# Beacon attention and soft-MoE slots on one core: pair 2's scores before the first attends, the tail's PSUM tiles, a weight load and dummy matmuls moved

## The chip, the cores and the metric

One NeuronCore of a Trainium2 chip runs the whole program. The metric is the time of one execution on the device in microseconds. Six executions of the kernel before took 194.52 to 196.42 us, with a median of 196.32. One execution was profiled; its trace gives the start and length of every instruction and every transfer.

## The reference

Causal attention with 16 beacon keys in front, for 8 batches of 8 heads, followed by a soft mixture of experts over all 4608 tokens:

```python
# q, k, v: (8, 8, 576, 64); beacon_k, beacon_v: (8, 8, 16, 64), float32
k_all = np.concatenate([beacon_k, k], axis=2)
v_all = np.concatenate([beacon_v, v], axis=2)
scores = scale * np.matmul(q, k_all.transpose(0, 1, 3, 2))
scores = np.where(causal, -1000000000.0, scores)      # beacons are never masked
a = softmax(scores)                                    # over the keys
x = np.matmul(a, v_all)                                # -> (4608, 512): tokens, heads * 64
logits = x @ phi                                       # phi (512, 32): 8 experts * 4 slots
d = softmax(logits, axis=0)                            # over the tokens (dispatch)
slot_input = (d.T @ x).reshape(8, 4, 512)
for e in range(8):
    h = np.maximum(slot_input[e] @ w1[e], 0.0)         # w1 (8, 512, 1024)
    slot_out[e] = h @ w2[e]                            # w2 (8, 1024, 512)
c = softmax(logits, axis=1)                            # over the slots (combine)
out = c @ slot_out.reshape(32, 512)                    # (4608, 512) float32
```

## The kernel before

The schedule is written by hand: each engine runs its instructions in the order of the program text, and waits are placed where tiles overlap. The unit of work is a pair of heads: 32 pairs, `n` from 0 to 31, four pairs (`g` = 0 to 3) to a batch `b`.

**One pair.** `load_pair` (L90) reads q and k of a pair as float32, 288 KB each, on SP's queue, into one of five slots; pair `m + 5` is issued (`load_more`, L407) as soon as PE has turned pair `m`. `transp(n, i)` (L253) turns q (`i` = 0) or k (`i` = 1) with 18 small PE transposes into a `tr` tile of PSUM, of which there are two, and a copy brings it to `qT` or `kT`: DVE (L271) or, for k of pairs 0, 2, 3, 4 and 7, ACT (L269). The first 16 columns of `kT` are the pair's beacon keys from `bkT` (L256 on ACT, L258 on DVE or POOL); `beacons` (L242) makes `bkT`, for batch 0 ahead of the loop and for the others at n = 3, after POOL has doubled them (L205).

`score(n, st)` (L275) computes the transposed scores of a pair in four steps into the PSUM tiles `scs[0]` and `scs[1]` by turns; ACT takes the exponential into `ex[n]` (L289) and POOL zeroes the causal triangle (L291). `attend_blocks` (L298) multiplies 15 blocks of `ex` for each head with v and a column of ones, which gives the sums of the softmax, into the PSUM tile `av`: head 0 in its first half, head 1 in its second. `normalize` (L310) is a reciprocal (L314) and a multiplication (L315) on DVE, into `xb`. `xt_piece` (L333) turns `xb` back through a `tr` tile into `xT`, copied by DVE (L343). `logit_piece` (L345), `dt_piece` (L359) and `si_products` (L383) are the routing of a finished batch: logits and their exponential, its transposition, and the sums for the slots.

**v and the weights** go through POOL's queue as casting loads to float16: v in pieces of 32 partitions (`load_v` L112, `load_tail` L143), the experts' weights in 32 pieces of 512 KB (`load_w` L176). DVE turns v (`turn_v` L154, `turn_tail` L158, both L151) before it can be used. POOL's DMA semaphores come round every eight loads: a load waits until the one eight before it has landed. POOL runs its loads and its affine selects in one order. Of the weights, one piece follows at the end of each iteration as `want` (L540) says: none at n = 0, then one each at n = 1 to 5, none at n = 6.

**The loop's order.** An iteration is `score(n, 0)`, `score(n, 1)`, the attend of head 0 of an earlier pair, `score(n, 2)`, the turning of k of the next pair, `score(n, 3)`, the attend of head 1 and `normalize`. In the first iterations the attends lag by two pairs; at n = 4 two pairs are attended and the lag becomes one. `transp(m, 0)` of the next q stands after `score(n, 1)` up to n = 4 and after `score(n, 0)` from n = 5 on. At n = 4 and 5 two `xt_piece` follow each other (L463). `warm` (L237) issues dummy matmuls on a tile that nobody reads: six and two ahead of the loop, two at n = 1, four at n = 2.

**The tail** (from L553). The last pair's heads are attended in `scs[0][:, 0]` and `av[:, 1]`, each normalized by itself (`normalize_head`, L320). Then come the last logits (L564) into `scs[1]`, the folding of the slots' sums (`fold_si`, L398) into `scs[0][:, 1]`, `col_sums` (L420), which adds the combine weights of a token into columns of `av[:, 0]`, three dummies (L582), `dt_piece`, and the slots' inputs into `siz`. The experts run in four steps of two experts: `first_layer(p)` (L609) into `scs[0][:, 0]` or `av[:, 1]` by turns and a relu on ACT (L618), `turn_hidden(p)` (L620) with a copy on DVE (L624), `second_layer(p)` (L626) into `sop`, which is `av[:, 0]`. At p = 1 `col_sums(7, NG)` and its factors on DVE (L549, L551) follow. `soh` (L648) scales the result, and 37 matmuls (L660) with copies by ACT and DVE write the output, 9.4 MB on SP's queue.

Of the kernel before, what the change touches and what calls it, by code (L numbers as in the profile page):

```python
# [17 lines left out]
def kernel(  # L18
# [190 lines left out]
        load_v(0, qd)  # L209
    for i in range(3):  # L210
        load_tail(0, i)
    idh = const.tile([P, P], F16, name="idh")
    ones = const.tile([P, 1], F16, name="ones")
    nc.vector.memset(ones[:, :], 1.0)
# [80 lines left out]
    def attend_head(n, a):  # L295
        attend_blocks(n, a, av[:, a, :], [(c, i) for i in range(NCH) for c in range(i + 1)])
# [10 lines left out]
                vchunk(b, 2 * g + a, c, kn),  # L307
                start=(c == 0), stop=(c == i))

    def normalize(n):  # L310
        b, g = divmod(n, H // 2)
        r5 = sml.tile([P, 2, NCH], FP, name="r5", tag="r5")
        avv = av[:, :, 0:NCH * DD].rearrange("p a (i d) -> p a i d", d=DD)
        nc.vector.reciprocal(out=r5[:, :, :], in_=avv[:, :, :, D])  # L314
        nc.vector.tensor_tensor(  # L315
            out=xb[b % 2][:, :, 2 * g:2 * g + 2, :].rearrange("p i a d -> p a i d"),
            in0=avv[:, :, :, 0:D],
            in1=r5[:, :, :].unsqueeze(3).broadcast_to([P, 2, NCH, D]), op=AL.mult)

    def normalize_head(n, a, src):  # L320
        b, g = divmod(n, H // 2)
        r5 = sml.tile([P, NCH], FP, name="r5h", tag="r5h")
        avv = src[:, 0:NCH * DD].rearrange("p (i d) -> p i d", d=DD)
        nc.vector.reciprocal(out=r5[:, :], in_=avv[:, :, D])
        nc.vector.tensor_tensor(
            out=xb[b % 2][:, :, 2 * g + a, :], in0=avv[:, :, 0:D],
            in1=r5[:, :].unsqueeze(2).broadcast_to([P, NCH, D]), op=AL.mult)

    xT = {}
    dT = {}  # L330

    def xt_piece(n):
        b, g = divmod(n, H // 2)  # L333
        if g == 0:
            xT[b] = exq.tile([P, NDC, U], F16, name="xT", tag="xT", bufs=2)
        tp = ps_tr.tile([P, NCH, P], F16, name="tr", tag="tr")
        for i in range(NCH):
            m = P if i < 4 else UL
            nc.tensor.transpose(  # L339
                tp[:, i, 0:m],  # L340
                xb[b % 2][0:m, i, 2 * g:2 * g + 2, :].rearrange("p h d -> p (h d)"),
                idh[0:m, 0:m])
        nc.vector.tensor_copy(out=xT[b][:, g, :],  # L343
                              in_=tp[:, :, :].rearrange("p i u -> p (i u)")[:, 0:U])

    def logit_piece(b, hf):
        lp = ps_tr.tile([P, 512], FP, name="tr", tag="tr")
# [49 lines left out]

    def fold_si(h):  # L398
        if h == 0:
            fsp[0] = scs[0][:, 1, 0:NDC * NSL].rearrange("p (c s) -> p c s", c=NDC)  # L400
        for c in (2 * h, 2 * h + 1):
            x = siacc[:, 256 * h:256 * h + 256].rearrange("p (f r) -> p f r", r=2)
            nc.tensor.matmul(fsp[0][:, c, :], x[:, :, c % 2], fold[:, :], start=True, stop=True)
        if h == 1:
            nc.vector.tensor_copy(out=siT[:, :, :], in_=fsp[0])
# [25 lines left out]
    transp(0, 1)  # L431
    warm(1)
    nc.vector.tensor_copy(out=idh[:, :], in_=idb[:, :])
    wl = 0
    for n in range(NP):
        b, g = divmod(n, H // 2)
        score(n, 0)
        m = n + 1 if n < 6 else n + 2
        if 5 <= n and m < NP:
            transp(m, 0)  # L440
        if n == NP - 1:
            dt_piece(b - 1)
        score(n, 1)
        if n == NP - 1:
            add_si(si_products(b - 1))
        if n < 5:
            transp(m, 0)
        for x, y in {1: ((0, 0), (0, 1)), 3: ((1, 1),), 4: ((1, 0), (1, 2)), 6: ((2, 0), (2, 1)),
                     7: ((2, 2),), 8: ((2, 3),)}.get(n, (divmod(n + 3, 4),) if n > 8 else ()):
            if x < B:  # L450
                turn_v(x, y)
        if 13 <= n < 17:
            turn_tail(1, n - 13)
        if n == 2:
            warm(4)
        if 2 <= n < 5:
            attend_head(n - 2, 0)
        elif n >= 5:
            if n >= 8 and g == 0:
                col_sums(b - 2, b - 1)  # L460
            attend_head(n - 1, 0)
        if n >= 4:
            for x in {4: (0, 1), 5: (2, 3)}.get(n, (n - 2,)):  # L463
                xt_piece(x)
        score(n, 2)
        if n == 3:
            beacons(1, B)
        if m < NP:
            if n == 1:
                warm(2)  # L470
            transp(m, 1)
            if n > 0:
                load_more(m)
        score(n, 3)
        if n == 0:
            hold(3)
            load_pair(3)
            nc.sync.dma_start(out=bkf[:, 1:B, :], in_=bks[:, 1:B, :])
            load_pair(4)
            load_more(0)  # L480
            load_more(1)
            nc.sync.dma_start(out=phif[:, :, :], in_=moe_phi.rearrange("(c p) e -> p c e", p=P))
        if n == 0:
            load_v(1, 0)
        if n == 1:
            for y in range(1, 4):
                load_v(1, y)
            turn_v(0, 2)
            turn_v(0, 3)
            for y in range(4):  # L490
                turn_tail(0, y)
        if n >= 2:
            x = n - 2 if n < 5 else n - 1
            attend_head(x, 1)
            normalize(x)
        if n == 4:
            turn_v(1, 3)
            attend_head(3, 0)
            attend_head(3, 1)
            normalize(3)  # L500
        if n == 5:
            for i in range(2):
                transp(7, i)
            load_more(7)
        if 6 <= n < NP - 1 and g == 3:
            dt_piece(b - 1)
        if n >= 5 and g in (1, 2):
            logit_piece(b - 1, g - 1)
        if n >= 8 and g == 0:
            add_si(si_products(b - 2))  # L510

        if n == 4:
            nc.gpsimd.tensor_copy(out=phih[:, :, :, :],
                                  in_=phif[:, :, :].unsqueeze(2).broadcast_to([P, NDC, 4, NSL]))
        if n == 2:
            for r in range(2):
                double_beacons(nc.gpsimd, r, 1, B)
        if n == 12:
            nc.gpsimd.memset(siz[:, :, :, :], 0.0)
        if n == 16:  # L520
            nc.gpsimd.tensor_copy(out=fold[:, :], in_=idb[:, 0:NSL])
            for z in range(1, 4):
                nc.gpsimd.tensor_tensor(out=fold[:, :], in0=fold[:, :],
                                        in1=idb[:, NSL * z:NSL * z + NSL], op=AL.add)
            nc.gpsimd.tensor_scalar(out=fold[:, :], in0=fold[:, :], scalar1=2.0 ** -8,
                                    scalar2=None, op0=AL.mult)
        if n == 3:
            for qd in range(4):
                load_v(2, qd)
        if n == 4:  # L530
            load_bv(2)
        x, y = divmod(n - 4, 4)
        if n >= 4 and x + 3 < B:
            for qd in ((0,), (1, 2), (3,), ())[y]:
                load_v(x + 3, qd)
            if y == 2:
                load_bv(x + 3)
        if 8 <= n < 11:
            load_tail(1, n - 8)
        want = n if n < 6 else n - (n - 2) // 4 if n < 24 else 18 + 9 * (n - 23) // 5  # L540
        while wl < min(want, NPC):
            load_w(wl)
            wl += 1
# [8 lines left out]

    L = B - 1  # L553

    avl = [scs[0][:, 0, :], av[:, 1, :]]
    for a in range(2):
        attend_blocks(NP - 1, a, avl[a], [(c, 4) for c in range(NCH)])
    xt_piece(NP - 2)
    for a in range(2):
        attend_blocks(NP - 1, a, avl[a], [(c, i) for i in (3, 2, 1, 0) for c in range(i + 1)])  # L560
        normalize_head(NP - 1, a, avl[a])
    lps = [scs[1][:, hf, 0:S // 2] for hf in range(2)]

    def last_logits(ts):  # L564
# [4 lines left out]
                                 xT[L][:, t, o:o + S // 2],  # L569
                                 start=(t == 0), stop=(t == NDC - 1))  # L570

    last_logits(range(NDC - 1))
    fold_si(0)
    xt_piece(NP - 1)
    fold_si(1)
    last_logits([NDC - 1])
    for hf in range(2):
        o = Nb + L * S + hf * (S // 2)
        nc.scalar.activation(eLh[:, o:o + S // 2], lps[hf], AF.Exp)
    col_sums(6, 7)  # L580
    for _ in range(3):
        nc.tensor.matmul(scs[0][:, 1, :], idh[:, :], xT[L][:, 0, 0:512], start=True, stop=True)  # L582
    dt_piece(L)
    ds = siz[:, :, :, :]
    for hf in range(2):
        sp = si_half(L, hf)
# [20 lines left out]
    EP = E // 2  # L607

    def first_layer(p):  # L609
        hp = av[:, 1, :] if p % 2 else scs[0][:, 0, :]  # L610
        for c in range(NDC):
            for z in range(4):
                e = 2 * p + z // 2
# [21 lines left out]
    for p in range(EP + 2):  # L635
        if p < EP:
            first_layer(p)
        if 0 < p <= EP:
            turn_hidden(p - 1)
        if p == 1:  # L640
            col_sums(7, NG)
            col_sum_factors()
        if p > 1:
            second_layer(p - 2)
    soh = const.tile([P, Dm], F16, name="soh")
# [55 lines left out]
```

The softmax here doesn't subtract the row's maximum and nothing guards it: scores larger than these inputs give would overflow.

## Time and profile before

| | us |
|---|---|
| median of 6 runs | 196.32 |
| lowest and highest | 194.52, 196.42 |
| profiled execution | 196.42 |
| its span, first to last instruction | 194.7 |
| PE busy | 157.3 |
| DVE busy | 137.6 |
| ACT busy | 129.0 |
| POOL busy | 111.1 |

Busy times are those of one engine within the span; they overlap, so they don't add up to it. Of PE, matmuls and weight loads are counted apart (weight loads 104.6 us). The granted clock of PE was 0.961 of full speed in the mean. The transfers read 62.65 MB and wrote 9.44 MB. The chain that ended last, by engine:

```profile
PE 62%; DVE 10%; DMA 7%; issue 6%; POOL 3%; ACT 3%; SPq 1%; DVEq 0%
```

"issue" is time in which an engine waited for nothing that the profile shows, and a q after an engine's name is its queue. The loop runs from about 6.5 us to 149 us, the routing and the experts of the tail to 166.7 us, the output to the end. Loads take long to land since many are under way at once, which the page's list of issues shows (size of one, median from issue to landing):

```profile
arena<-in_moe_w_dram POOLq DMA_DIRECT2D x32, 512.0 KB, 9.3
arena<-in_q_dram SPq DMA_DIRECT2D x32, 288.0 KB, 12.8
arena<-in_k_dram SPq DMA_DIRECT2D x31, 288.0 KB, 13.5
```

### The profile page before, as it was taken

The page shows a single profiled execution, that of the slowest core. Times are in us where ns is not written, and L with a number is a line of the kernel's source. Part 1 is how long each engine was busy: PE and PEld are TensorE (multiplying, and loading weights), DVE is VectorE, ACT ScalarE, POOL GpSimd, SP SyncE. Part 2 cuts the span into 40 slices and gives each one's busy share as a digit, 9 for nine tenths or more (in the row PEclk, how much of TensorE's full clock was granted, in tenths as well). Part 3 has the DMA queues.
Part 4 walks back from the last instruction along what each step waited for, and adds up shares of the span by engine and source line. Part 5 has one row for each costly group of instructions (what it writes and reads, how often), then busy time and mean ns, then how long its engine had stood idle before and what let it go on. Part 6 is the DMA issues. An engine that isn't in the chain of part 4 may idle for free.

```text
span 194.7 us, 7200 instructions
## 1 busy us (share of the span) xinstructions
PE 157.3 (81%) x3063; PEld 104.6 (54%) x3065; DVE 137.6 (71%) x286; ACT 129.0 (66%) x189; POOL 111.1 (57%) x285
## 2 busy tenths in 40 slices
PE   6668857899997999999899998988987889787000
PEld 2435645677575766666676775666655654332000
DVE  5573397889986899899788899877755552699000
ACT  2793964698696788878977987887896122499000
POOL 8687675868788598659957876666756200000000
PEclk9996999999999999999999999999999999999755
DMA  5999999999999999999999999999999980199995
GB/s 198 266 265 349 251 296 291 257 263 260 308 267 263 257 287 292 263 282 296 253 271 266 276 260 280 236 220 216 215 216 210 204 163 3 56 403 417 416 426 226
DMA packets 20464, 50.84 MB, mean 261 GB/s; under 512 B 5456, under 2 KB 5456, under 8 KB 19408
## 3 DMA queue, kind: packets, MB, share of 16 engines
q0 software_dynamic: 8048, 21.74, 56.6%
q1 hardware_dynamic: 12240, 28.35, 39.6%
q8 instruction: 24, 0.39, 0.7%
q10 hardware_dynamic: 144, 0.29, 0.5%
q14 instruction: 8, 0.07, 0.1%
HBM read 62.65 MB, written 9.44 MB: 370 GB/s over the span
## 4 chain that ended last, share of the span: by engine, by line
PE 62%; DVE 10%; DMA 7%; issue 6%; POOL 3%; ACT 3%; SPq 1%; DVEq 0%
PE av L304 18%; PE sc L282 15%; PE tr L265 11%; DVE arena L664 4%; PE tr L339 4%; DMA arena<-in_moe_w_dram 4%; DMA arena<-in_k_dram 3%; PE tr L350 3%; DVE xb L315 2%; PE av L629 2%; PE tr L388 2%; ACT ex L289 1%; POOL ex L291 1%; PE av L422 1%; PE sc L615 1%
## 5 line engine op out<-in xcount | busy, mean ns | idle before, releaser
L289 ACT ACTIVATE ex<-sc 128x736 f16<-128x736 f32 (+1 forms) x124 | 101.9, 868 | 24.7 <-PE sc L282 23.1
L291 POOL TENSOR_SCALAR_AFFINE_SELECT ex<-ex 128x256 f16<-128x256 f16 (+1 forms) x155 | 57.6, 401 | 33.8 <-ACT ex L289 33.2
L282 PE MATMUL sc<-qT,kT 64*128 64x336 bf16 (+5 forms) x384 | 45.4, 287 | 5.4 <-POOL kT L258 1.2
L304 PEld LDWEIGHTS <-ex 128*128 128x128 f16 (+1 forms) x930 | 35.8, 106 | 17.6 <-issue 16.8
L304 PE MATMUL av<-vh,ex 128*128 128x65 f16 (+1 forms) x854 | 39.6, 197 | 5.8 <-issue 3.5
L265 PE MATMUL tr<-idb,arena 64*64 64x64 bf16 x1152 | 31.2, 197 | 2.8 <-issue 1.6
L265 PEld LDWEIGHTS <-arena 64*64 64x64 bf16 x1152 | 23.9, 110 | 12.1 <-issue 8.9
L271 DVE COPY qT<-tr 128x576 bf16<-128x576 bf16 x32 | 24.0, 751 | 6.9 <-PE tr L265 6.1
L315 DVE TENSOR_TENSOR xb<-av,r 128x640 f16<-128x640 f32 x31 | 25.5, 824 | 1.1
L282 PEld LDWEIGHTS <-kT 64*128 64x128 bf16 (+1 forms) x384 | 15.7, 98 | 18.4 <-issue 9.3
L271 DVE COPY kT<-tr 128x576 bf16<-128x576 bf16 x27 | 20.4, 755 | 5.8 <-PE tr L265 5.7
L151 DVE STREAM_TRANSPOSE vh<-vbuf 128x256 f32<-128x256 f32 x32 | 20.4, 657 | 2.0 <-DMA arena<-in_moe_w_dram 1.8
L183 POOL DMA_DIRECT2D arena<-in_moe_w_dram x32 | 18.0, 564 | 0.2
L343 DVE COPY xT<-tr 128x592 f16<-128x592 f16 x32 | 13.9, 441 | 3.7 <-PE tr L339 3.6
L127 POOL DMA_DIRECT2D vbuf<-in_v_dram x27 | 15.2, 569 | 0.0
L662 ACT ACTIVATE arena<-fp,rc 128x512 f32<-128x512 f32 (+1 forms) x18 | 11.3, 673 | 5.4 <-PE fp L660 4.6
L314 DVE RECIPROCAL r<-av 128x10 f32<-128x10 f32 x31 | 6.9, 221 | 11.1 <-PE av L304 10.7
L339 PE MATMUL tr<-idh,xb 128*128 128x128 f16 (+1 forms) x160 | 13.4, 215 | 0.0
L664 DVE TENSOR_SCALAR arena<-fp,rc 128x512 f32<-128x512 f32 (+1 forms) x19 | 12.6, 731 | 0.4 <-PE fp L660 0.4
L660 PE MATMUL fp<-soh,eLh 128*128 128x512 f16 (+1 forms) x37 | 10.7, 371 | 2.4 <-ACT arena L662 1.6
L350 PE MATMUL tr<-xT,phih 128*128 128x288 f16 x56 | 9.2, 285 | 0.7 <-ACT kT L269 0.7
L339 PEld LDWEIGHTS <-xb 128*128 128x128 f16 (+1 forms) x160 | 9.7, 99 | 0.1
(102 smaller groups left out, 136.1 us busy)
## 6 DMA issues: line engine op xcount, KB each, us to landing
arena<-in_moe_w_dram POOLq DMA_DIRECT2D x32, 512.0 KB, 9.3
arena<-in_q_dram SPq DMA_DIRECT2D x32, 288.0 KB, 12.8
arena<-in_k_dram SPq DMA_DIRECT2D x31, 288.0 KB, 13.5
out_dram<-arena SPq DMA_DIRECT2D x8, 1024.0 KB, 9.3
vbuf<-in_v_dram POOLq DMA_DIRECT2D x30, 128.0 KB, 7.2
arena<-in_v_dram POOLq DMA_DIRECT2D x4, 128.0 KB, 7.6
out_dram<-arena SPq DMA_DIRECT2D x2, 256.0 KB, 3.0
out_dram<-arena SPq DMA_DIRECT2D x1, 512.0 KB, 3.2
```

The lines of the kernel that those rows point to most:

```text
L127: nc.gpsimd.dma_start(out=vbuf[b % 2][32 * qd:32 * qd + 32, :], in_=bass.AP(tensor=v.tensor, offset=v.offset + lo, ap=[hs_, cs_, [1, TK * ...
L151: nc.vector.transpose(out=dst[:, e], in_=src.bitcast(FP).rearrange("p (j e) -> p e j", j=TK)[:, e])
L183: nc.gpsimd.dma_start(out=arena[:, wloc[m]:wloc[m] + WP], in_=src)
L265: nc.tensor.transpose(tp[po:po + 64, j, :], hi, idb[po:po + 64, po:po + 64])
L271: nc.vector.tensor_copy(out=dst, in_=src)
L282: nc.tensor.matmul(sc[0:kn, a, col:col + un], kT[n % 3][64 * a:64 * a + 64, P * c:P * c + kn], qT[n % 3][64 * a:64 * a + 64, u0:u0 + un], ...
L289: nc.scalar.activation(e, sc[:, :, 0:w], AF.Exp, scale=scale)
L291: nc.gpsimd.affine_select(out=e[0:m, :, o:o + m], in_=e[0:m, :, o:o + m], compare_op=AL.is_ge, fill=0.0, base=0, pattern=[[0, 2], [1, m]], ...
L304: nc.tensor.matmul(dst[0:m, i * DD:(i + 1) * DD], ex[n][0:kn, o + a * w:o + a * w + m], vchunk(b, 2 * g + a, c, kn), start=(c == 0), stop= ...
L315: nc.vector.tensor_tensor(out=xb[b % 2][:, :, 2 * g:2 * g + 2, :].rearrange("p i a d -> p a i d"), in0=avv[:, :, :, 0:D], in1=r5[:, :, :]. ...
L339: nc.tensor.transpose(tp[:, i, 0:m], xb[b % 2][0:m, i, 2 * g:2 * g + 2, :].rearrange("p h d -> p (h d)"), idh[0:m, 0:m])
L664: nc.vector.tensor_scalar(out=osb[:, j, c], in0=fp_[:, c], scalar1=rc[:, i:i + 1], scalar2=None, op0=AL.mult)
```

## The change

- In the loop: the four and two dummies at n = 2 and n = 1 go. The attend of pair 0's head 0 moves at n = 2 from between `score(2, 1)` and `score(2, 2)` to behind `score(2, 3)`, where that of head 1 follows it.
- `transp(6, 0)` moves from n = 5 (after `score(5, 0)`) to n = 4, before the attends of pair 3.
- The `xT` copies of pairs 0 to 3, made at n = 4 and 5, move from DVE to ACT.
- `load_w(0)` is issued ahead of the loop, behind the tails of v; each weight piece up to the fifth is issued one iteration sooner, and n = 5 issues none.
- In the tail: both heads of the last pair are attended in `scs[0]`, block row 4 first, then 3 to 1, then 0, and normalized together; `xt_piece(30)` follows with its copy on ACT; the last logits are split into three groups around `fold_si` and `xt_piece(31)`; `fold_si` writes to `av[:, 1]`.
- Two dummies follow `dt_piece`. The first layers use `scs[0][:, 0]` and `scs[1][:, 0]` by turns. At p = 1 the column sums and their factors come before `turn_hidden(0)`.

```diff
@@ -209,6 +209,7 @@
         load_v(0, qd)
     for i in range(3):
         load_tail(0, i)
+    load_w(0)
     idh = const.tile([P, P], F16, name="idh")
     ones = const.tile([P, 1], F16, name="ones")
     nc.vector.memset(ones[:, :], 1.0)
@@ -307,29 +308,20 @@
                 vchunk(b, 2 * g + a, c, kn),
                 start=(c == 0), stop=(c == i))
 
-    def normalize(n):
+    def normalize(n, src=av):
         b, g = divmod(n, H // 2)
         r5 = sml.tile([P, 2, NCH], FP, name="r5", tag="r5")
-        avv = av[:, :, 0:NCH * DD].rearrange("p a (i d) -> p a i d", d=DD)
+        avv = src[:, :, 0:NCH * DD].rearrange("p a (i d) -> p a i d", d=DD)
         nc.vector.reciprocal(out=r5[:, :, :], in_=avv[:, :, :, D])
         nc.vector.tensor_tensor(
             out=xb[b % 2][:, :, 2 * g:2 * g + 2, :].rearrange("p i a d -> p a i d"),
             in0=avv[:, :, :, 0:D],
             in1=r5[:, :, :].unsqueeze(3).broadcast_to([P, 2, NCH, D]), op=AL.mult)
 
-    def normalize_head(n, a, src):
...
     xT = {}
     dT = {}
 
-    def xt_piece(n):
+    def xt_piece(n, act=False):
         b, g = divmod(n, H // 2)
         if g == 0:
             xT[b] = exq.tile([P, NDC, U], F16, name="xT", tag="xT", bufs=2)
@@ -340,8 +332,11 @@
                 tp[:, i, 0:m],
                 xb[b % 2][0:m, i, 2 * g:2 * g + 2, :].rearrange("p h d -> p (h d)"),
                 idh[0:m, 0:m])
-        nc.vector.tensor_copy(out=xT[b][:, g, :],
-                              in_=tp[:, :, :].rearrange("p i u -> p (i u)")[:, 0:U])
+        src = tp[:, :, :].rearrange("p i u -> p (i u)")[:, 0:U]
+        if act:
+            nc.scalar.activation(xT[b][:, g, :], src, AF.Copy)
+        else:
+            nc.vector.tensor_copy(out=xT[b][:, g, :], in_=src)
 
     def logit_piece(b, hf):
         lp = ps_tr.tile([P, 512], FP, name="tr", tag="tr")
@@ -397,7 +392,7 @@
 
     def fold_si(h):
         if h == 0:
-            fsp[0] = scs[0][:, 1, 0:NDC * NSL].rearrange("p (c s) -> p c s", c=NDC)
+            fsp[0] = av[:, 1, 0:NDC * NSL].rearrange("p (c s) -> p c s", c=NDC)
         for c in (2 * h, 2 * h + 1):
             x = siacc[:, 256 * h:256 * h + 256].rearrange("p (f r) -> p f r", r=2)
             nc.tensor.matmul(fsp[0][:, c, :], x[:, :, c % 2], fold[:, :], start=True, stop=True)
@@ -431,12 +426,12 @@
     transp(0, 1)
     warm(1)
     nc.vector.tensor_copy(out=idh[:, :], in_=idb[:, :])
-    wl = 0
+    wl = 1
     for n in range(NP):
         b, g = divmod(n, H // 2)
         score(n, 0)
         m = n + 1 if n < 6 else n + 2
-        if 5 <= n and m < NP:
+        if 6 <= n and m < NP:
             transp(m, 0)
         if n == NP - 1:
             dt_piece(b - 1)
@@ -451,9 +446,7 @@
                 turn_v(x, y)
         if 13 <= n < 17:
             turn_tail(1, n - 13)
-        if n == 2:
-            warm(4)
-        if 2 <= n < 5:
+        if 3 <= n < 5:
             attend_head(n - 2, 0)
         elif n >= 5:
             if n >= 8 and g == 0:
@@ -461,13 +454,11 @@
             attend_head(n - 1, 0)
         if n >= 4:
             for x in {4: (0, 1), 5: (2, 3)}.get(n, (n - 2,)):
-                xt_piece(x)
+                xt_piece(x, n < 6)
         score(n, 2)
         if n == 3:
             beacons(1, B)
         if m < NP:
-            if n == 1:
-                warm(2)
             transp(m, 1)
             if n > 0:
                 load_more(m)
@@ -491,10 +482,13 @@
                 turn_tail(0, y)
         if n >= 2:
             x = n - 2 if n < 5 else n - 1
+            if n == 2:
+                attend_head(x, 0)
             attend_head(x, 1)
             normalize(x)
         if n == 4:
             turn_v(1, 3)
+            transp(6, 0)
             attend_head(3, 0)
             attend_head(3, 1)
             normalize(3)
@@ -537,7 +531,7 @@
                 load_bv(x + 3)
         if 8 <= n < 11:
             load_tail(1, n - 8)
-        want = n if n < 6 else n - (n - 2) // 4 if n < 24 else 18 + 9 * (n - 23) // 5
+        want = n + 1 if n < 5 else 5 if n < 6 else n - (n - 2) // 4 if n < 24 else 18 + 9 * (n - 23) // 5
         while wl < min(want, NPC):
             load_w(wl)
             wl += 1
@@ -552,13 +546,12 @@
 
     L = B - 1
 
-    avl = [scs[0][:, 0, :], av[:, 1, :]]
-    for a in range(2):
-        attend_blocks(NP - 1, a, avl[a], [(c, 4) for c in range(NCH)])
-    xt_piece(NP - 2)
-    for a in range(2):
-        attend_blocks(NP - 1, a, avl[a], [(c, i) for i in (3, 2, 1, 0) for c in range(i + 1)])
-        normalize_head(NP - 1, a, avl[a])
+    avl = scs[0]
+    for rows in ((4,), (3, 2, 1), (0,)):
+        for a in range(2):
+            attend_blocks(NP - 1, a, avl[:, a, :], [(c, i) for i in rows for c in range(i + 1)])
+    normalize(NP - 1, avl)
+    xt_piece(NP - 2, True)
     lps = [scs[1][:, hf, 0:S // 2] for hf in range(2)]
 
     def last_logits(ts):
@@ -569,18 +562,25 @@
                                  xT[L][:, t, o:o + S // 2],
                                  start=(t == 0), stop=(t == NDC - 1))
 
-    last_logits(range(NDC - 1))
+    last_logits([0, 1])
     fold_si(0)
     xt_piece(NP - 1)
+    last_logits([2])
     fold_si(1)
-    last_logits([NDC - 1])
+    last_logits([3])
     for hf in range(2):
         o = Nb + L * S + hf * (S // 2)
         nc.scalar.activation(eLh[:, o:o + S // 2], lps[hf], AF.Exp)
     col_sums(6, 7)
-    for _ in range(3):
-        nc.tensor.matmul(scs[0][:, 1, :], idh[:, :], xT[L][:, 0, 0:512], start=True, stop=True)
+
+    def warm_tail(k):
+        for _ in range(k):
+            nc.tensor.matmul(scs[0][:, 1, :], idh[:, :], xT[L][:, 0, 0:512],
+                             start=True, stop=True)
+
+    warm_tail(3)
     dt_piece(L)
+    warm_tail(2)
     ds = siz[:, :, :, :]
     for hf in range(2):
         sp = si_half(L, hf)
@@ -607,7 +607,7 @@
     EP = E // 2
 
     def first_layer(p):
-        hp = av[:, 1, :] if p % 2 else scs[0][:, 0, :]
+        hp = scs[p % 2][:, 0, :]
         for c in range(NDC):
             for z in range(4):
                 e = 2 * p + z // 2
@@ -635,11 +635,11 @@
     for p in range(EP + 2):
         if p < EP:
             first_layer(p)
-        if 0 < p <= EP:
-            turn_hidden(p - 1)
         if p == 1:
             col_sums(7, NG)
             col_sum_factors()
+        if 0 < p <= EP:
+            turn_hidden(p - 1)
         if p > 1:
             second_layer(p - 2)
     soh = const.tile([P, Dm], F16, name="soh")
```

More of the change, by code (lines that the diff above doesn't have):

```diff
@@ L318, in normalize @@
             in1=r5[:, :, :].unsqueeze(3).broadcast_to([P, 2, NCH, D]), op=AL.mult)
-    def normalize_head(n, a, src):
[L321 to L327, printed above, removed]
     xT = {}
     dT = {}
-    def xt_piece(n):
+    def xt_piece(n, act=False):
         b, g = divmod(n, H // 2)
```

## The prediction, made before the change was run

> **What bounds the kernel now.** I read four views in this order: the page's slices, the transfers of single stretches, the chain that ended last, and the timeline around the lines the diff touches. The slices first:
>
> ```profile
> span 194.7 us, 7200 instructions
> PEclk9996999999999999999999999999999999999755
> DMA  5999999999999999999999999999999980199995
> ```
>
> Each digit is 4.87 us. The transfers are full from the second slice to the 32nd, stop for three slices and are full again for the output. So the input phase has no spare transfer time: whatever is read earlier pushes something else later. Who is pushed shows in two stretches, 12 to 20 us and 20 to 45 us (packets, megabytes, share of 16 engines):
>
> ```profile
> q1 hardware_dynamic: 2078, 2.34, 86.7%
> q0 software_dynamic: 258, 0.31, 20.8%
> ...
> q0 software_dynamic: 1348, 3.37, 67.8%
> q1 hardware_dynamic: 1982, 3.33, 38.0%
> ```
>
> q1 carries q and k (issued by SP), q0 carries v and the expert weights (issued by POOL). From 20 us on q and k get only 38%.
>
> The chain of waits, early part (start, length, what):
>
> ```profile
> 16.61 8.00 DMA arena<-in_moe_w_dram
> 24.63 0.67 DVE vh L151
> 27.79 1.09 DVE vh L151 x2
> 28.89 0.32 DVE xT L343
> 29.25 0.47 PE tr L265 x18
> ```
>
> DVE stands at `turn_v(1, 1)` until a POOL load lands. The chain names the weight piece, but the turn needs the v loads issued just ahead of it on the same queue; the last of those was issued at 16.09 and landed at 24.60. After it the chain is DVE to 29.2, then PE to the tail. The timeline at the touched lines:
>
> ```profile
> 18.77 0.94 ACT L289 ACTIVATE arena<-sc 128x928 f16<-128x928 f32 x1 [3.27 <-PE sc L282]
> 26.23 0.11 PEld L282 LDWEIGHTS <-kT 64*128 64x128 bf16 x4 [1.40 <-POOL kT L258]
> 28.77 0.80 DVE L343 COPY xT<-tr 128x592 f16<-128x592 f16 x2
> 29.25 0.47 PE L265 MATMUL tr<-idb,arena 64*64 64x64 bf16 x18 [0.67 <-DVE xT L343]
> 150.34 0.30 PE L304 MATMUL av<-vh,ex 128*80 128x65 f16 x4 [0.60 <-DVE xb L315]
> 159.20 0.40 PE L422 MATMUL av<-ones,eLh 32*128 32x1 f16 x8 [0.37 <-ACT hbuf L618]
> 163.44 1.05 PE L629 MATMUL av<-arena,hbuf 128*32 128x512 f16 x16 [0.37 <-ACT hbuf L618]
> ```
>
> The bracket is idle time before the instruction and who ended it. The first is the gap in front of pair 2's third score, the last three are waits of the tail.
>
> **Pair 2's scores ahead of the attends: nothing.** ACT loses 3.27 us at 18.77 because PE first runs four dummies and an attend. With these behind, `score(2, 2)` and `(2, 3)` can start as soon as q and k of pair 3 are turned, up to 3.27 us sooner. But the next pairs pass through DVE's turn at 24.63: `beacons`' copies follow it in DVE's queue (25.17), then POOL's beacon keys (25.99), then `score(4, 0)` at 26.23. The landing at 24.60 does not move with the scores, so the gain becomes idle time in front of it. If that cover were gone it would be worth up to 3.27.
>
> **Dummies in the loop (6 removed): nothing**, since they lie ahead of the same wait: 1.37 us for three of them at 15.55. The clock is their risk. The granted clock averages 0.62 between 16 and 20 us, although PE was 2.30 of 4 us busy between 12 and 16. The Trainium skill ("TensorE: Matmul & The Clock Gate", Part 1) says that the clock halves after an idle window of about 3.4 us. By that rule removing dummies costs nothing, as no window becomes idle; by the row a 58% busy stretch was enough, and 25 to 30 us is just as thin (2.99 of 5). A halved stretch as long as the one seen (about 3.4 us) adds at most half its length, 1.7 us: bounds 0 and 1.7, taken 0, since the clock held in that thin stretch.
>
> **First weight piece ahead of the loop: +0.8 us.** `load_w(0)` joins POOL's queue behind the v tails. In order, one piece is issued one iteration sooner up to n = 4, and that of n = 5 disappears. Its size in transfer time: late in the loop pieces of 512 KB land 2.45 us apart with nothing else running. The sixteen engines are full, so q and k fall behind by 2.45 us of transfer time until the place of the missing piece, issued at 39.15 and landing at 49.23, gives it back. At a share of 38% that is 2.45 / 0.38 = 6.4 us on the clock. Slack against it, landing to use: pair 8's q, issued 18.46, takes 14.2 and lands at 32.7, is turned at 39.35: 6.6. Pair 9's q, issued 22.09, takes 15.2, lands at 37.3, is turned at 43.24: 5.9; its k 39.2 to 45.06: 5.8. So PE waits 0.6 us (6.4 less 5.8). Upper bound: between 34 and 45 us q and k get only 31.4%, 2.45 / 0.314 = 7.8, a wait of 2.0. Lower bound 0. POOL itself: its DMA semaphores come round every eight loads, so the third v load now waits for that piece to land and may go out up to 1 us later than 16.09; the affine selects queued behind it have slack, the turn at 24.63 has none: 0 to 1.0. A later turn also gives q and k time, so the two don't add; I take 0.8 for both, the estimate's 0.6 and a little of the second.
>
> **xT copies of n = 4 and 5 to ACT, `transp(6, 0)` forward: -0.3 us.** DVE loses four copies of 0.42; the 0.67 wait at 29.25 falls to about 0.1, since ACT is free at 27.96 and a copy of that size takes 0.65 there (L269, 128x576). That is -0.55 in n = 4. In n = 5 ACT has two copies between its exps: 2 x 0.65 = 1.3 in a gap of 0.92 (before 35.65), which hands back about 0.3. `transp(6, 0)`, 0.47 of PE, moves into PE's 1.17 us wait at 31.81. Bounds -0.6 (all of it) and +0.4 (ACT leads). q of pair 11 can be issued some 2.5 us sooner, behind others in the same queue: nothing.
>
> **Tail.** *Attends of pair 31 in one tile*: the wait of 0.60 goes, but row 0 still needs the last affine select (150.32 + 0.41). The two per-head normalizations end at 152.71; one of 0.22 + 0.82 after matmuls that end near 151.25 ends near 152.4. PE, with two logit products fewer ahead of it, reaches `xt_piece(31)` near 152.5 in place of 152.76: -0.25, bounds 0 and -0.6. ACT, idle 3.94 us there, takes the copy of pair 30: nothing. *First layer out of av*: col_sums and second_layer no longer wait for ACT's read of av's other half: 2 x 0.37 = 0.74; the column sums (0.33 to 0.40) now stand in front of the turn, where PE's loads wait 0.42 for ACT, so up to 0.4 more. Taken -0.8, bounds -0.3 and -1.15. DVE's factors (0.20 + 0.38) now precede the first hidden copy; that is needed only after the next first layer, about 1.3 us later. *Two dummies after dt_piece*: 0.82 / 3 = 0.27 each, 0.55 in PE's wait of 0.46 at 155.81: +0.1, bounds 0 and 0.3; the clock was full there, so no gain. The last weight piece (issued 151.37, 10.5 to land, 161.9) is needed past 164, so an earlier second layer finds it.
>
> A second page speaks against the -0.8: "PSUM — Partial Sum Buffer" (bank collisions) asks for a guard by bank and quadrant only, and the two halves of av are two banks. By that rule alone PE need not have waited and the new tiles save nothing; the two rows show it waiting, so the row decides.
>
> **Sum**: 0 + 0 + 0.8 - 0.3 - 0.25 - 0.8 + 0.1 = -0.45. The profiled execution took 196.42, 1.7 around its span of 194.7, and stands 0.1 above the median of 196.32. Against the median: 195.9.
>
> **Rivals.** *Faster: q and k arrive in time.* If POOL's queue takes its turn without holding q and k back (slack 5.8 against 6.4 is close), the 0.8 drops out: 196.32 - 1.25 = 195.1, and with all bounds favourable (-0.6 - 0.6 - 1.15) 194.0. For it: before, no turn of pairs 8 to 12 waits for a transfer; against it, the full DMA slices. *Slower: the early piece starves q and k.* 2.0 us at pairs 8 and 9 and 1.0 at the turn of v, without overlap, and the ACT gain lost: 196.32 + 3.0 - 1.05 + 0.1 = 198.4. It decides from a loss of 2.2 upward before n = 10 (1.25 and 0.98). For it: 31.4%; against it: a waiting PE also issues POOL's next loads later. *The hoist works as meant:* 3.27 less, 192.7; against it the landing at 24.60, which nothing in the change brings forward.
>
> **How the numbers follow.** What a measurement of this kernel can tell is about 0.5%, 0.98 us: 195.3 to 197.3 counts as no change. Forecast (tail gain, partly given back early): 42%. Arriving in time: 34%, and the hoist working: 3%; both are faster: 0.37. Starved or a halved clock: 21%. The forecast's own range, from its terms, is 195.3 to 196.9. The range of all, leaving out the hoist and the far end of starving: 194.3 to 198.2.
>
> **What would show it.** Right: PE waits on `in_q` or `in_k` loads between 20 and 47 us; DVE's turn still starts at 24.6 to 25.6; second layers without the 0.37 waits, and from the first `siz` to the end of the second layer 9.3 us in place of 10.1. Wrong: `score(4, 0)` complete well before 26 us, or no wait on q and k at all, or a granted clock below 1 after 20 us.

## The result and the profile after

| | before | after |
|---|---|---|
| median | 196.24 us (72 runs) | 195.9 us (35 runs) |
| ratio, 95% interval | | 0.9998 [0.9976, 1.0021] |
| profiled execution | 196.42 us | 194.75 us |
| its span | 194.7 us | 192.8 us |

The change made no difference that can be measured, as forecast. The medians take in all executions; the ratio and its interval, here and below, only those within 1.5% of the fastest of their kernel. The 72 executions of the kernel before spread over 7.3 us and the 35 of the changed kernel over 5.0, so the totals of two profiled executions say little; stretches of the tail repeat within 0.02 us, and those carry the reading below.

The page's slices of the changed kernel, 4.82 us each:

```profile
span 192.8 us, 7196 instructions
PEclk9955699999999999999999999999999999999655
DMA  5999999999999999999999999999999991399993
```

The transfers are as full as before, but the stop ahead of the output is shorter (slices at 1 and 3, before 8, 0 and 1), and the clock is low in the third to fifth slice, where before had one 6. The transfers at 12 to 20 us and at 20 to 45 us (packets, megabytes, share of 16 engines):

```profile
q1 hardware_dynamic: 1682, 1.82, 66.2%
q0 software_dynamic: 310, 0.62, 40.0%
...
q0 software_dynamic: 1364, 3.38, 67.9%
q1 hardware_dynamic: 2085, 3.25, 38.2%
```

The early weight piece shows in the first pair of lines: POOL's queue takes 40.0% in place of 20.8%, q and k get 66.2% in place of 86.7%. After 20 us nothing has changed. The chain by engine, and five links of it in order of time (start, length, what):

```profile
PE 59%; DMA 16%; DVE 5%; issue 4%; ACT 4%; POOL 2%; SPq 1%; DVEq 0%
```

```profile
10.75 7.59 DMA arena<-in_k_dram
18.39 0.69 PE tr L266 x18
19.62 1.88 PE av L305 x30
...
27.65 16.74 DMA arena<-in_q_dram
45.16 0.60 PE av L305 x15
```

In place of the weight load and DVE's turn, which stood in the chain up to 29 us, there are now loads of k and q: k of pair 3, which ends at 18.34, and q of pair 9, which ends at 44.39. The share of DMA in the chain went from 7% to 16%. That is one execution: in the second profile of this kernel (e9 below) the chain has 31% of DMA and runs through the early weight piece (7.88 to 18.42) and a v load (to 25.14) to the same q of pair 9 (to 44.79). The timeline at the touched lines:

```profile
17.14 0.69 PE L266 MATMUL tr<-idb,arena 64*64 64x64 bf16 x18 [1.31 <-DMA arena<-in_q_dram]
18.37 0.94 ACT L290 ACTIVATE arena<-sc 128x928 f16<-128x928 f32 x1 [1.76 <-PE sc L283]
24.31 0.67 DVE L151 STREAM_TRANSPOSE vh<-vbuf 128x256 f32<-128x256 f32 x1 [0.69 <-DMA vbuf<-in_v_dram]
28.02 1.22 ACT L337 ACTIVATE xT<-tr 128x592 f16<-128x592 f16 x2 [0.36 <-PE tr L331]
28.73 0.47 PE L266 MATMUL tr<-idb,arena 64*64 64x64 bf16 x18
44.44 0.47 PE L266 MATMUL tr<-idb,arena 64*64 64x64 bf16 x18 [1.00 <-DMA arena<-in_q_dram]
156.88 0.42 PE L417 MATMUL av<-ones,eLh 32*128 32x1 f16 x8
161.03 1.05 PE L629 MATMUL av<-arena,hbuf 128*32 128x512 f16 x16
```

The first line is new: PE stands at q of pair 3. The gap in front of pair 2's third score (second line) shrank from 3.27 to 1.76 us. DVE's turn (third line) still waits for its v load. The turning of pair 5's k at 28.73 has lost its wait of 0.67, the turning of pair 9's q at 44.44 has got one of 1.00. The last two lines, the column sums and a second layer, stand without a bracket where each had 0.37 us.

Two stretches of the tail can be compared directly, both read from the trace: from the first exponential of pair 31 to the first weight load of the first layer, 10.87 us before and 10.54 after; from there to the start of `soh` (L648), 10.20 and 9.27. Together -1.26 us.

### The profile page after: what moved, and what is told of

Read it like the earlier page. It is cut to its first block, busy times and chain, and to the rows that moved or that the text cites. A ratio compares the mean times of both kernels' runs of the same rounds, so it can differ in the third digit from the quotient of the medians.

```text
span 192.8 us, 7196 instructions
## 1 busy us (share of the span) xinstructions
PE 158.9 (82%) x3061; PEld 105.3 (55%) x3061; DVE 135.3 (70%) x279; ACT 131.7 (68%) x194; POOL 111.6 (58%) x285
## 4 chain that ended last, share of the span: by engine, by line
PE 59%; DMA 16%; DVE 5%; issue 4%; ACT 4%; POOL 2%; SPq 1%; DVEq 0%
PE av L305 16%; PE sc L283 14%; PE tr L266 11%; DMA arena<-in_q_dram 9%; DMA arena<-in_k_dram 7%; PE tr L331 3%; ACT ex L290 2%; PE tr L345 2%; DVE arena L664 2%; PE av L629 2%; PE sc L615 2%; PE tr L383 2%; PE fp L660 2%; PE av L417 1%; POOL ex L292 1%
## 5 line engine op out<-in xcount | busy, mean ns | idle before, releaser
L283 PE MATMUL sc<-qT,kT 64*128 64x336 bf16 (+5 forms) x384 | 46.8, 298 | 2.6 <-ACT ex L290 1.3
L305 PE MATMUL av<-vh,ex 128*128 128x65 f16 x840 | 39.2, 198 | 4.2 <-issue 2.3
L266 PE MATMUL tr<-idb,arena 64*64 64x64 bf16 x1152 | 31.9, 200 | 5.3 <-DMA arena<-in_q_dram 2.7
L266 PEld LDWEIGHTS <-arena 64*64 64x64 bf16 x1152 | 24.7, 113 | 14.7 <-issue 6.8
L151 DVE STREAM_TRANSPOSE vh<-vbuf 128x256 f32<-128x256 f32 x32 | 20.5, 658 | 1.5 <-DMA vbuf<-in_v_dram 0.7
L339 DVE COPY xT<-tr 128x592 f16<-128x592 f16 x27 | 11.8, 436 | 2.6 <-PE tr L331 2.5
```

Of the source, the lines that this page charges most:

```text
L151: nc.vector.transpose(out=dst[:, e], in_=src.bitcast(FP).rearrange("p (j e) -> p e j", j=TK)[:, e])
L266: nc.tensor.transpose(tp[po:po + 64, j, :], hi, idb[po:po + 64, po:po + 64])
L283: nc.tensor.matmul(sc[0:kn, a, col:col + un], kT[n % 3][64 * a:64 * a + 64, P * c:P * c + kn], qT[n % 3][64 * a:64 * a + 64, u0:u0 + un], ...
L305: nc.tensor.matmul(dst[0:m, i * DD:(i + 1) * DD], ex[n][0:kn, o + a * w:o + a * w + m], vchunk(b, 2 * g + a, c, kn), start=(c == 0), stop= ...
```

## The experiments

In the expectations A is the prediction's own sum, the other letters are rivals that the texts describe. Ratios are to the kernel before on the same chip, with 95% intervals.

**Which half of the change does what.** The tail alone (e1):

```diff
+ the helpers and everything behind the loop as in the changed kernel
  loop, dummies and weight loads as before
```

> The loop, the dummies and the weight loads of before, the tail of the change (last pair in one tile, first layers in tiles of their own, column sums ahead of the first turn, two dummies). Theory A (the tail gains, the early weight piece gives it back): 1.2 us less than before, about 195.0, and from the first siz to the end of the second layer about 9.2 us where before had 10.1. Rival B (the end is set by the output's or the weights' transfers, a shorter tail is waited for again): within 0.3 us of before, 196.2, with the same 9.2 us.

Measured: 193.34 us, ratio 0.9879 [0.9824, 0.9934] (6 runs), larger than expected. The two stretches of the tail were 10.54 and 9.28 us, exactly those of the changed kernel. Since these account for 1.26 us (0.64%) and the ratio for 2.4, the same kernel was run again later (e5):

> The same kernel as e1_tail (before's loop and weights with the changed tail), beside the next three on one chip. Theory A (the loop's edits without the early weight piece are worth about nothing to -0.3 us, and 0.9879 was partly scatter): ratio 0.991 to 0.995, the 0.9947 of the changed kernel without the early piece within the interval. Theory D (removing the loop's dummies or hoisting the scores costs about 1 us, so that the tail alone is the better kernel): 0.986 to 0.990 again.

Measured: 194.86 us, 0.9943 [0.9901, 0.9984] (12 runs), the stretches 10.55 and 9.28. That is the gain that the stretches show; the part of 0.9879 beyond it did not repeat.

The weight piece alone, on the kernel before (e2):

```diff
     for i in range(3):
         load_tail(0, i)
+    load_w(0)
...
-    wl = 0
+    wl = 1
...
-        want = n if n < 6 else ...
+        want = n + 1 if n < 5 else 5 if n < 6 else ...
```

> Before with load_w(0) ahead of the loop and each weight piece up to the fifth one iteration sooner; nothing else. Theory A: q and k land 5 to 7 us later between 17 and 45 us, PE waits 1 to 2.5 us for them, 0.8 to 1.5 us more than before: 197.0 to 197.7. Rival C (the piece fills a gap of POOL's queue and costs nothing; the loss, if any, is the clock's): 196.2, and no waits of PE for q and k beyond before's 1.5 us in total.

Measured: 196.19 us, 1.0012 [0.9973, 1.0051]: 0.2 us, where the prediction's term was 0.8. Its profile shows the delay of theory A all the same: q of pairs 8 and 9 landed at 37.71 and 42.40 us (before: 32.70 and 37.30), and PE's matmuls waited 2.9 us for q and k in the first 60 us (before: 0.3). Of these, 1.29 us were for q of pair 3 at 17.05, though no scores are moved forward here. That q landed at 17.0 to 17.7 us in all six profiles with one early piece and at 14.2 to 15.9 in the seven without, so the new wait at 17.14 in the changed kernel comes with the piece. The line of e2:

```profile
17.05 0.69 PE L266 MATMUL tr<-idb,arena 64*64 64x64 bf16 x18 [1.29 <-DMA arena<-in_q_dram]
```

The changed kernel without the early piece (e3, the same lines put back):

> The change with the weight pieces issued where before issues them. Theory A: the waits on q and k between 20 and 47 us go, 194.7 to 195.1, 0.8 to 1.2 less than the whole change. Rival C: as the whole change, 195.9.

Measured: 194.5 us, 0.9947 [0.9909, 0.9985]. Against the changed kernel's 0.9998 the piece costs 0.0051, uncertain by 0.0044: 1.0 us, near the prediction's 0.8. q of pairs 8 and 9 landed at 32.59 and 37.27, where the changed kernel has 39.42 and 44.39, and no matmul waited for q or k between 20 and 47 us. The two answers on the cost differ, so the piece was doubled in the changed kernel (e4):

```diff
+    load_w(0)
+    load_w(1)
...
+    wl = 2
...
+        want = n + 2 if n < 4 else 5 if n < 6 else ...
```

> The change with two weight pieces ahead of the loop, the places at n = 4 and n = 5 empty. Theory A: q and k fall behind by 4.9 us of transfer time in place of 2.45, PE waits some 2 us more than in the whole change: 197.5 to 198.5. Rival C: 195.9.

Measured: 198.35 us, 1.0105 [1.0047, 1.0164]. The second piece costs 0.0107, 2.1 us, with intervals well apart. The waits of this kernel between 0 and 60 us (who waits, for whom: us in total, times, longest):

```profile
PE tr L267 <- DMA arena<-in_q_dram: 4.0, 3, 2.2
PE tr L267 <- DMA arena<-in_k_dram: 2.8, 3, 1.9
DVE vh L151 <- DMA vbuf<-in_v_dram: 1.9, 1, 1.9
```

The same lines of the changed kernel:

```profile
PE tr L266 <- DMA arena<-in_q_dram: 2.7, 3, 1.3
PE tr L266 <- DMA arena<-in_k_dram: 0.8, 1, 0.8
DVE vh L151 <- DMA vbuf<-in_v_dram: 0.7, 1, 0.7
```

The waits of PE's matmuls for q and k grow from 3.5 us (2.6 in the second profile of the changed kernel, e9) to 6.8, DVE's for v from 0.7 (1.4 in e9) to 1.9, and `turn_v(1, 1)` starts at 26.64 instead of 24.31 (25.23 in e9). So a piece ahead of the loop does hold q, k and v back.

**The loop's edits, one by one, on the tail.** That the tail alone is worth 0.6% and the whole change nothing left the loop to be asked.

```diff
  e6: tail, and
-        if 5 <= n and m < NP:
+        if 6 <= n and m < NP:
...
-                xt_piece(x)
+                xt_piece(x, n < 6)
...
+            transp(6, 0)
```

> The changed tail plus the xT copies of pairs 0 to 3 on ACT and transp(6, 0) forward; dummies, attend order and weights as before. By the prediction's term -0.3 us against the tail alone: ratio 0.0015 below e5_tail_again, with bounds -0.6 and +0.4 us (0.003 below to 0.002 above). If the xT edit is what costs the changed loop about 1 us (theory D's other reading): 0.005 above e5_tail_again.

Measured: 194.96 us, 0.9955 [0.9908, 1.0002]; 0.0012 above the tail alone. The difference of two such ratios is uncertain by 0.006, so it can't be told from the -0.3 us of the prediction, nor from nothing.

```diff
  e7: tail, and
-        if n == 2:
-            warm(4)
-        if 2 <= n < 5:
+        if 3 <= n < 5:
             attend_head(n - 2, 0)
...
-            if n == 1:
-                warm(2)
...
+            if n == 2:
+                attend_head(x, 0)
```

> The changed tail plus the hoist of pair 2's scores and the six loop dummies removed; xT copies, transp(6, 0) and weights as before. Theory A: within 0.0025 of e5_tail_again (hoist and dummies are worth nothing, since DVE waits for the v load), with turn_v(1, 1) still starting at 23 to 25.5 us. Theory D: 0.004 to 0.007 above e5_tail_again, with a longer half-clock stretch in the first 30 us than in e5_tail_again.

Measured: 195.74 us, 0.9994 [0.9949, 1.004], 0.0051 above the tail alone (uncertain by 0.006), with `turn_v(1, 1)` at 24.27. The half-clock time before 40 us was 20.5 us in its profile against 17.1 in the tail's, which alone decides nothing. The suspects are the moved scores and the dummies; the dummies alone were put back:

```diff
  e8: the changed kernel, and
+        if n == 2:
+            warm(4)
...
+            if n == 1:
+                warm(2)
```

> The changed kernel with the six loop dummies back in their places (four after score(2, 1), two at n = 1). Theory A: within 0.0025 of the changed kernel's 0.9998, the four dummies (1.4 us) hidden by the waits for q and k of pair 3 that the hoisted scores meet. Theory D, if the clock is the cause: 0.994 to 0.996, and less half clock between 9 and 25 us than the changed kernel's 13.65 us.

Measured: 194.53 us, 0.9941 [0.9902, 0.998]: the gain that theory D expected, 0.0057 below the changed kernel. The half-clock stretch in its profile was as long as the changed kernel's (13.65 us), against what D expected of it. To rule out a difference between chips, both were run again side by side (e9 and e10), with two more:

> The changed kernel itself, beside the next three on one chip. Theory D (the six dummies that went cost about 1 us through the clock): ratio to before 0.998 to 1.002 and a mean granted clock over its executions of 0.930 to 0.937. If 0.9998 against the 0.9941 of the kernel with dummies was a difference between chips: 0.994 here.

Measured: 196.22 us, 0.9976 [0.9934, 1.0017]; granted clock, mean over all its executions, 0.929.

> The changed kernel with the six loop dummies back, again. Theory D: 0.004 to 0.007 below e9_changed_again, mean granted clock 0.940 to 0.947. Theory A (dummies worth nothing): within 0.0025 of e9_changed_again.

Measured: 194.12 us, 0.9906 [0.9867, 0.9945]; mean clock 0.945. Again 0.0070 below the changed kernel. The two comparisons, weighted by their uncertainties (worked out from the intervals: 0.0057 within 0.0045, 0.0070 within 0.0057), give 0.0062 within 0.0035: the six dummies that went cost 1.2 us, give or take 0.7.

```diff
  e11: e10 without the early weight piece
-    load_w(0)
```

> The changed kernel with the six loop dummies back and no weight piece ahead of the loop. If the early weight piece costs 0.8 us by itself as predicted: 0.004 below e10_dummies_again, about 0.990. If it costs only where the dummies are gone (0.0053 of the ratio between the changed kernel with and without it, but 0.0012 when it alone is added to before): within 0.002 of e10_dummies_again.

Measured: 194.05 us, 0.9911 [0.9868, 0.9954]: where the dummies stay, no cost of the early piece is seen (0.0005, uncertain by 0.006). Against the changed kernel, dummies and piece together are worth 0.0087, uncertain by 0.005: 1.7 us. e11 and e6 differ only by the moved scores of pair 2; e11 is lower by 0.0044, uncertain by 0.006, so these can't be told from nothing.

```diff
  e12: e10, and
-            if n == 1:
-                warm(2)
+            if n < 2:
+                warm(2 + 2 * n)
```

> The changed kernel with the six dummies back and four more: two ahead of k's turning at n = 0, and four instead of two at n = 1, to bring a 3.4 us stretch of PE above 93% busy before 20 us. Theory D: mean granted clock 0.946 to 0.955 and a ratio 0.001 to 0.003 below e10_dummies_again. Rival (dummies at half clock take 0.47 to 0.63 us each on PE's path): 0.002 to 0.005 above it.

Measured: 195.03 us, 0.9948 [0.9909, 0.9987], mean clock 0.951. The clock rose as D expected, and the time rose too, by 0.0042, as the rival expected, though that is uncertain by 0.0055. Its profile shows the four dummies of n = 1 taking 1.02 us together at 12.20, full clock. More clock bought with more dummies brought no gain here.

**Where the dummies' 1.2 us are.** One part is visible in every profile: from the first output transfer on. The issues of output in the changed kernel, and in the kernel with its dummies back (e10); the last number is the median from issue to landing:

```profile
out_dram<-arena SPq DMA_DIRECT2D x8, 1024.0 KB, 9.8
out_dram<-arena SPq DMA_DIRECT2D x2, 256.0 KB, 3.4
out_dram<-arena SPq DMA_DIRECT2D x1, 512.0 KB, 4.8
```

```profile
out_dram<-arena SPq DMA_DIRECT2D x8, 1024.0 KB, 9.4
out_dram<-arena SPq DMA_DIRECT2D x2, 256.0 KB, 3.0
out_dram<-arena SPq DMA_DIRECT2D x1, 512.0 KB, 3.2
```

Both begin to write at nearly the same time (166.17 and 166.20). In the changed kernel the first transfer lands 0.4 us sooner (168.68 against 169.09), the second 1.2 us later (171.06 against 169.83) and the last 0.5 us later (191.80 against 191.29). The queues at 168.3 to 169.7 us in the changed kernel, and at 165.5 to 167.5 us in e10:

```profile
q1 hardware_dynamic: 153, 0.51, 102.5%
q8 instruction: 1, 0.02, 4.8%
```

```profile
q1 hardware_dynamic: 83, 0.17, 23.0%
q8 instruction: 1, 0.02, 3.8%
```

q8, which the profile calls instruction, fetches code: 16 KB in one packet, which holds one of the sixteen engines for 1.07 us here (0.9 to 1.5 in the other profiles). In the changed kernel it runs while the output fills all sixteen; in e10 it starts before the first output is issued (166.02) and ends at 167.22, when the output's own packets have run for 0.2 us. In all 14 profiles the last such packet starts when 6071 to 6077 of PE's recorded instructions have begun, so its place is a place in PE's program. Kernels with the dummies have 65 to 67 instructions left behind it (e12 77), kernels without 53 to 55, twelve fewer for six matmuls and six weight loads. With the dummies gone, that place lies twelve instructions nearer to the end, inside the output. From issue of the first output to the landing of the last, the five profiles without the dummies took 25.54 to 25.64 us, the nine with them 24.75 to 25.16. The nine sort by the same packet: 24.75 to 24.94 in the four where it ended before the output's first packet started, 25.10 to 25.16 in the five where it ran 0.2 to 0.3 us into the output. e8 and e10 are one kernel and took 24.78 and 25.10. No run moved the fetch alone, but it orders all 14 profiles, so 0.5 us (against e10) to 0.9 us (against e8) of the dummies' worth is put down to it.

The rest of the 1.2 us, 0.3 to 0.7, would lie in the loop; with 1.2 uncertain by 0.7, it is not clear of nothing. The profiles don't show it: pair 31's first exponential started at 144.50 and 144.49 us in the two of the changed kernel, at 145.69 and 144.52 in the two with its dummies back. The mean granted clock was 0.925 to 0.938 in the five sets of executions without the dummies and 0.942 to 0.951 in all others. Among executions of one kernel (193 of those that the ratios compare, in 16 sets) a clock lower by 0.01 went with 0.34 us more, give or take 0.12; the 0.009 and 0.013 between the kernels of the two comparisons would make 0.3 and 0.4 us. That fits the rest, but a late load makes an execution longer and PE's windows thinner alike, so the rest is not shown to be the clock's.

## Why the prediction was right, and where it wasn't

Forecast was -0.45 us; the ratio stands for -0.04, between -0.47 and +0.41. Its terms did less well than the total. The tail gained 0.3 us more than its term, and the dummies cost 1.2, give or take 0.7, where the term was nothing. With -1.26 for the tail and +1.7 for dummies and early piece together, -0.5 is left for the scores and the xT copies (predicted -0.3), within the noise. That errors of opposite sign brought the total so near is in part luck.

- *Pair 2's scores ahead, nothing*: nothing speaks against it (e11 against e6: -0.9 us, uncertain by 1.3). The gap on ACT shrank, and the turn at 24.31 (24.27 in e7) still waited for its v load, as in the timeline above. What the step did not name: the moved scores need q and k of pair 3, and with the early piece q came so late that PE waited 1.31 us at 17.14.
- *Dummies, nothing, bounds 0 and 1.7*: wrong in size, 1.2 us. The step looked for a halved clock only. The bound of 1.7 holds the size, but not for the reason given: 0.5 to 0.9 us of it goes with the code fetch, which the step did not see. Nor did the rule that it quotes hold here, that the clock halves after an idle window: windows with PE 26 to 54% busy were enough (last section). Of the clock it had the mark that would show it wrong, "a granted clock below 1 after 20 us": the clock of the changed kernel came back at 23.04. The value taken, 0, rested on one profile in which the clock held in a thin stretch; the last section shows what that was worth.
- *Early weight piece, +0.8*: the delay is shown. q of pairs 8 and 9 landed 6.7 and 7.1 us later than before (worked out: 6.4), and e3 and e4 move it with the piece. The cost in the changed kernel was 1.0, uncertain by 0.9. Where PE waits is less settled: 0.42 us at 39.47 and 1.00 at 44.44 in one profile, as the step had it, but in the second profile of the same kernel no matmul waits for q or k between 20 and 47 us. Both wait for q of pair 3 at 17 us (1.31 and 1.61), for which the step has no term. And where the dummies stay, the piece costs 0.2 (e2) or nothing (e11). Why the same delay is hidden there was not settled; the intervals would also allow one cost of 0.4 us throughout.
- *xT copies on ACT, -0.3*: the row predicted to shrink did, 0.67 to nothing in front of 28.73. As a time it could not be measured (e6).
- *Tail, -0.95*: the stretches give -1.26, the same within 0.02 us in all twelve profiles with the changed tail. The attends with the two dummies gave -0.33 (predicted -0.15), the first layer out of av -0.93 (predicted -0.8). The place where a page of the Trainium skill, "PSUM — Partial Sum Buffer" (bank collisions), spoke against the -0.8 was decided rightly by the rows: the two waits of 0.37 went with the shared tile.
- The sum: -1.26 in the tail and +0.5 in the output leave +0.7 for the loop, to reach -0.04. The loop's share is uncertain by 0.4. The prediction had -0.95, nothing and +0.5.
- The rivals: with q and k in time the kernel would have taken 195.1. That is about what e3 took without the piece (194.5). Starvation at 198.4 came true only with two pieces (198.35). Of the 3.27 us that the moved scores were to bring no run shows anything (3.27 less than the forecast's 195.87 is 192.6, not 192.7).

A version that beats both kernels came out: the changed kernel with its six dummies back, 0.9941 and 0.9906 in its two measurements and 0.9911 without the early piece. It is not told apart from the changed tail alone (0.9879 and 0.9943).

## What to carry to other kernels

A removed instruction can have a cost that its own duration doesn't show: where the next code fetch falls once the program is shorter. What it did for the clock may be another; that part was not shown here. Of work moved ahead, look up when its own inputs land, not only what stands behind it. And where executions scatter by 2%, compare stretches that repeat (here within 0.02 us), and use totals only over many runs; one profile of a waiting engine is one execution, and a second may put the wait elsewhere.

## What the runs showed of the hardware that was not expected

**The granted clock.** It moves in windows of 3.41 us whose phase differs from execution to execution: up to 50 us every halved stretch of the 14 profiles is 3.41, 6.83, 10.24 or 13.65 us long, one to four windows, and they start at different times. The changed kernel's windows from 5.97 us on (stretch: length, busy us of PE, PEld, DVE, ACT, POOL with their instructions, granted clock, share of the transfers, GB/s):

```profile
5.97:9.38 3.41, 1.88 (x47) 1.12 (x46) 1.36 (x4) 2.85 (x4) 2.27 (x7) 1.00 1.04 266
9.39:12.79 3.40, 2.77 (x43) 1.34 (x38) 1.24 (x3) 2.32 (x3) 1.81 (x5) 0.50 1.10 209
12.80:16.20 3.40, 2.08 (x28) 1.02 (x28) 3.40 (x8) 3.39 (x6) 3.40 (x9) 0.50 1.02 274
16.21:19.62 3.41, 2.42 (x42) 1.39 (x43) 1.67 (x3) 1.65 (x4) 3.33 (x8) 0.50 1.08 347
19.63:23.03 3.40, 3.40 (x62) 2.94 (x63) 1.21 (x3) 2.25 (x4) 2.24 (x6) 0.50 1.08 294
23.04:26.44 3.40, 3.10 (x66) 2.17 (x63) 2.59 (x6) 2.95 (x5) 1.54 (x6) 1.00 1.11 263
```

PE was 55% busy in the first window, and the clock halved. It stayed halved through windows of 81, 61 and 71%, and came back only after one that was 100% busy. Counted over the windows of all 14 profiles between 4 and 50 us: at full clock, a window at most 54% busy was followed by a halved one 12 times of 12, one of 55 to 65% 7 times of 14, one of 66% or more never. At half clock, windows of 34 to 91% were followed by another halved one 27 times of 27, of 93 to 95% by a full one 3 times of 5, and of 96% or more 16 times of 16. No idle window was needed to lose the clock, while one nearly full window was needed to get it back, so one thin window costs one to four windows. Where the grid falls in an execution can decide whether a thin stretch counts: the thin stretch of before at 25 to 30 us, 2.99 of 5 us busy, lay in windows of 67 and 66%, and the clock held. That is why a clock that held in one profile was poor evidence.

**The code fetch.** That six matmuls fewer at 10 to 20 us made the output at 167 us take at least 0.5 us longer was not foreseen by anything in the profile of before, although its own last fetch is in it, at 168.71, 0.12 us after the first output was issued.
